# Attention with a learned position bias, then expert routing: set-up tables by single logarithms, loads of the second sequence spread out, the last result in halves

## The chip, the core and the metric

The kernel runs on one core of a Trainium2 chip. The metric is device time in microseconds (us) of one execution. The engines are TensorE (PE, with its weight loads as PEld), VectorE (DVE), ScalarE (ACT), GpSimd (POOL) and SyncE (SP). POOL and SP also issue transfers (DMAs), each into a queue of its own.

## What is computed

Eight sequences of 576 tokens with 8 heads of 64 go through attention. A small network of 32 hidden units makes a position bias for each pair (i, j), and the 4608 resulting rows of 512 go to one of 8 experts each:

```python
psi_rel = np.log1p(np.abs(pos[:, None] - pos[None, :]))
psi_i = np.log1p(np.maximum(pos[:, None], 1.0))
x = (psi_rel / psi_i)[..., None]
h = np.maximum(x @ w1 + b1, 0.0)
bias = h @ w2                                   # one bias per head
scores = q @ k.T / sqrt(64) + bias
x = softmax(scores) @ v                         # rows of 8 heads x 64
for e in range(8):                              # each row belongs to one expert
    out[mask_e] = np.maximum(x[mask_e] @ w1[e], 0.0) @ w2[e]
```

## The kernel before

The work has three stages. PE, DVE and ACT run in the order in which the code is written (a manual schedule); the order on POOL and SP is set by the scheduler from the order of the code and from dependences.

**Set-up and bias.** `_setup_constants` (L127 to L197) makes a table L4 of log(1+|distance|), 1075 columns for the first eight row groups and 636 columns (tile li1, `last_table`) for the ninth. POOL writes whole numbers by iota, ACT takes Abs (L168, L191) and then Ln (L174, L192). For each query row `slope` holds w1/log(1+i): DVE makes the whole numbers (L169, L171), ACT takes Ln (L173), and `slopes(a, b)` takes the reciprocal and multiplies by w1 (L177, L178): 16 columns ahead of the first row, the other 128 in the midst of the first group, after its eighth row. `nb1` (L183) is the negated b1. `G.zero` is a tile of zeros that DVE fills (L162); SP writes it over the whole scratch tensor fire_x (9252 KB, L277) after the second group. `_phase_bias` then runs nine groups (ib) of 16 rows. A hidden row `hr` (128 x 576) is one instruction, on DVE as multiply and maximum (L218) or on ACT as Relu (L215: five rows of sixteen in the first two groups, then three). PE multiplies the rows by W2BIG (L238, L243), and ACT takes exp of the sums into the bias tables (biasM, L256; biasR, L251; the ninth group L264).

**Attention.** A unit is a block of scores: PE makes the scores into one of two PSUM buffers (L564, L570), ACT takes exp (L593), DVE multiplies by the bias table (L604), PE multiplies by v (vext for the first 512 keys, L629; vrag for the last 64, L627). PLAN, a table in the code, sets which unit's products follow which scores. Loads go out on POOL's queue in the order of the code (`G.issue`): `load_qk` (qn, kn; 512 KB each), `load_v` (vst), `load_last` (the last 64 rows of q and k, four small transfers) and `load_vrag` (two small ones). `start()` loads sequences 0 and 1 whole. qn, kn and vst take slots of a pool of six (`G.n4`); a slot comes free when its tile has been read for the last time (for vst that is `make_vext`, the copy L502). POOL also loads expert weights (w, L752) and scatters finished rows into fire_x (L671).

**Experts.** For each expert PE makes the hidden layer (L841) and the output (L813, eight matmuls of 512 columns for 128 rows, into the PSUM tile ops), DVE copies ops to res (L820), and POOL scatters res to the output (L821). The very last block of 128 rows is copied as two parts, one by DVE (L817) and one by ACT (L818).

Of the kernel before, what the change touches and what calls it, by code (L numbers as in the profile page):

```python
# [128 lines left out]
def _setup_constants(tc, G, w1, b1, w2):  # L129

    nc = tc.nc
    cst = G.cst
    w1col = cst.tile([P, 1], F32, tag="w1col", name="w1col")
    nc.sync.dma_start(out=w1col, in_=bass.AP(tensor=w1.tensor, offset=0, ap=[[0, 4], [1, 32], [1, 1]]))  # L140
    G.pb1 = cst.tile([P, 1], F32, tag="pb1", name="pb1")
    nc.sync.dma_start(out=G.pb1, in_=bass.AP(tensor=b1.tensor, offset=0, ap=[[0, 4], [1, 32], [1, 1]]))
    nc.scalar.preload_act_table_set("natural_log_exp_and_others")
    w2f = cst.tile([P, 32], F32, tag="w2f", name="w2f")
    nc.vector.memset(w2f, 0.0)
    for g in range(4):
        nc.sync.dma_start(out=w2f[32 * g: 32 * g + 32, 8 * g: 8 * g + 8], in_=w2[:, :])
    li = G.tmp.tile([P, W4], I32, tag="li", name="li")
    nc.gpsimd.iota(li, base=-C4, channel_multiplier=0, pattern=[[1, W4]])
    si = G.tmp.tile([P, NGR], I32, tag="si", name="si")  # L150

    nc.gpsimd.iota(si[:, 0:128], base=0, channel_multiplier=0, pattern=[[1, 4], [16, 32]])
# [27 lines left out]
    G.slopes = slopes  # L180
# [7 lines left out]
    G.second_layer = second_layer  # L188

    def last_table():  # L190
        nc.scalar.activation(out=lf1, in_=li1, func=AF.Abs, bias=gs[:, 3:4], scale=1.0)  # L191
        nc.scalar.activation(out=G.L4[:, W4:], in_=lf1, func=AF.Ln, bias=1.0, scale=1.0)  # L192
    G.last_table = last_table
    G.idn = cst.tile([P, P], F16, tag="idn", name="idn")
    make_identity(nc, G.idn)


def _phase_bias(tc, G, route, at, x_dram):
# [3 lines left out]
    with tc.tile_pool(name="fsb", bufs=1, side="right") as fsb, \  # L202
         tc.tile_pool(name="fps", bufs=1, space=bass.MemoryType.PSUM) as fps:

        def hidden(ib):
            hrl = []
            for k16 in range(16):
                if ib < 8:
                    r, a = ib // 2, 16 * (ib % 2) + k16
                    m, c0 = 32 * r + a, C4 - (16 * a + r)  # L210
                else:
                    m, c0 = 128 + k16, W4 + C1 - 4 * k16
                hr = fsb.tile([P, S], F16, tag="hr", name="hr", bufs=34)
# [216 lines left out]
class _Attention:  # L430
# [47 lines left out]
    def load_last(self, b, xs="qk"):  # L478
        nc = self.nc
        for nm in xs:  # L480
            x, src = "qk".index(nm), self.q if nm == "q" else self.k
            for h2 in range(2):
                self.G.issue(nc.gpsimd.dma_start(
                    out=self.last[b % 2][64 * h2: 64 * h2 + 64, :, x, 64 * h2: 64 * h2 + 64],
                    in_=src[b, h2::2, 512:576, :].rearrange("h p d -> p h d")))

    def load_v(self, b):
        nc = self.nc
# [49 lines left out]
    def scores(self, b, u, sc=None):  # L538
# [54 lines left out]
        nc.scalar.activation(out=ef[:, 0:n], in_=sf[:, 0:n], func=AF.Exp, bias=0.0, scale=0.125)  # L593
        if bias is None or j == 0:
            return None
        if j == 1:
# [95 lines left out]
    def run(self, route, late):  # L692
# [25 lines left out]
        for n in range((B + 1) * NU):  # L718
# [86 lines left out]
def _phase_moe(tc, G, moe_w1, moe_w2, x_dram, out):  # L805
# [4 lines left out]
    def second(hT, t0, e, idx):  # L810
        ops_ = mps.tile([P, DM], F32, tag="ops", name="ops", bufs=2)
        for fc in range(8):
            nc.tensor.matmul(out=ops_, lhsT=hT[:, fc, t0: t0 + 128], rhs=G.w.w2(e, fc),  # L813
                             start=(fc == 0), stop=(fc == 7))
        res = msb.tile([P, DM], F32, tag="res", name="res", bufs=RES)
        if (e, t0) == (E - 1, CAP - 128):
            nc.vector.tensor_copy(out=res[:, 0:256], in_=ops_[:, 0:256])  # L817
            nc.scalar.copy(out=res[:, 256:], in_=ops_[:, 256:])  # L818
        else:
            nc.vector.tensor_copy(out=res, in_=ops_)  # L820
        inst = nc.gpsimd.indirect_dma_start(  # L821
            out=out[:], out_offset=bass.IndirectOffsetOnAxis(ap=idx.bitcast(I32), axis=0),
            in_=res[:], in_offset=None, bounds_check=NTOK - 1, oob_is_err=False)
# [42 lines left out]
    for e in range(E):  # L866
# [67 lines left out]
def kernel(  # L934
# [25 lines left out]
    with tc.manual_schedule(engines={ET.PE, ET.DVE, ET.Activation}):  # L960
        with ExitStack() as att:
# [69 lines left out]
```

## Time and profile before

| | us |
|---|---|
| median of 3 runs | 356.21 (355.79 to 356.76) |
| profiled execution, its own time | 355.02 |
| its span, first to last instruction | 353.5 |
| PE busy | 324.5 (92%) |
| DVE busy | 247.3 (70%) |
| ACT busy | 246.3 (70%) |
| POOL busy | 167.7 (47%) |
| mean granted TensorE clock | 0.972 |

The profile is of one execution. The table gives shares of the whole span; the stages differ, so that each has to be read from its own stretch: from the start to about 50 us the bias tables are made, from there to about 205 us attention runs, and after that the experts.

### The profile page before, as it was taken

The page shows a single profiled execution, that of the slowest core. Times are in us where ns is not written, and L with a number is a line of the kernel's source. Part 1 is how long each engine was busy: PE and PEld are TensorE (multiplying, and loading weights), DVE is VectorE, ACT ScalarE, POOL GpSimd, SP SyncE. Part 2 cuts the span into 40 slices and gives each one's busy share as a digit, 9 for nine tenths or more (in the row PEclk, how much of TensorE's full clock was granted, in tenths as well). Part 3 has the DMA queues.
Part 4 walks back from the last instruction along what each step waited for, and adds up shares of the span by engine and source line. Part 5 has one row for each costly group of instructions (what it writes and reads, how often), then busy time and mean ns, then how long its engine had stood idle before and what let it go on. Part 6 is the DMA issues. An engine that isn't in the chain of part 4 may idle for free. (4 is left out here: it accounts for less than half of the span.)

```text
span 353.5 us, 9881 instructions
## 1 busy us (share of the span) xinstructions
PE 324.5 (92%) x4218; PEld 213.4 (60%) x4218; DVE 247.3 (70%) x436; ACT 246.3 (70%) x299; POOL 167.7 (47%) x211
## 2 busy tenths in 40 slices
PE   0489888999999999999999899999999999999993
PEld 0478855766666676666675564565655555565651
DVE  7999998999999999999999861206163616161211
ACT  7999989999999999999999953241424232323330
POOL 8370004727687676958483622506051515151323
PEclk9999757999999999999999999999999999999998
DMA  3999999999999899999999543999999999980202
GB/s 43 195 158 345 352 341 213 192 194 163 167 128 192 115 190 111 200 101 200 149 202 220 129 71 93 283 323 230 322 206 325 248 289 264 271 322 32 114 32 107
DMA packets 89349, 69.20 MB, mean 196 GB/s; under 512 B 43605, under 2 KB 77653, under 8 KB 89304
## 3 DMA queue, kind: packets, MB, share of 16 engines
q0 software_dynamic: 51984, 37.26, 65.0%
q1 hardware_dynamic: 37320, 31.30, 32.7%
q8 instruction: 33, 0.54, 0.6%
q14 instruction: 12, 0.10, 0.1%
HBM read 61.93 MB, written 24.70 MB: 245 GB/s over the span
## 5 line engine op out<-in xcount | busy, mean ns | idle before, releaser
L593 ACT ACTIVATE e<-sc 128x1024 f16<-128x1024 f32 x157 | 148.2, 1059 | 1.7
L874 ACT ACTIVATE hT<-hps 128x640 f16<-128x640 f32 x56 | 39.4, 704 | 78.1 <-PE hps L841 77.8
L820 DVE COPY res<-ops 128x512 f32<-128x512 f32 x39 | 27.0, 692 | 91.1 <-PE ops L813 90.1
L821 POOL DMA_INDIRECT out_dram<-res,ids x40 | 44.9, 1123 | 89.8 <-DVE res L820 73.3
L604 DVE TENSOR_TENSOR e<-e,biasM 128x2048 f16<-128x2048 f16 x64 | 72.9, 1149 | 1.6 <-ACT e L593 1.5
L813 PE MATMUL ops<-w,hT 128*128 128x512 f16 x320 | 70.5, 379 | 0.0
L629 PE MATMUL pu<-vext,e 128*128 128x65 f16 (+1 forms) x1280 | 64.8, 194 | 0.0
L841 PE MATMUL hps<-xT,w 128*128 128x320 f16 x448 | 62.0, 299 | 0.0
L629 PEld LDWEIGHTS <-e 128*128 128x128 f16 (+1 forms) x1280 | 56.1, 101 | 8.8 <-issue 6.8
L841 PEld LDWEIGHTS <-w 128*128 128x128 f16 x448 | 43.8, 98 | 18.1
L813 PEld LDWEIGHTS <-hT 128*128 128x128 f16 x320 | 31.2, 98 | 36.5 <-ACT hT L853 0.3
L564 PE MATMUL sc<-qkT 64*128 64x512 f16 x252 | 49.7, 391 | 3.8 <-ACT e L593 3.6
L671 POOL DMA_INDIRECT fire_x<-xt,posi x32 | 40.1, 1253 | 15.3 <-issue 7.6
L218 DVE TENSOR_SCALAR hr<-L,slope,nb 128x576 f16<-128x576 f16 x113 | 41.4, 433 | 0.1
L238 PE MATMUL eb<-W2BIG,hr 128*128 128x32 f16 x576 | 24.0, 192 | 14.6 <-DVE W2BIG L187 10.1
L627 PE MATMUL pu<-vrag,e 128*128 128x130 f16 (+1 forms) x160 | 35.7, 223 | 0.2 <-ACT e L593 0.2
L238 PEld LDWEIGHTS <-hr 128*128 128x128 f16 x576 | 21.5, 115 | 17.8 <-POOL vrag L450 6.7
L215 ACT ACTIVATE hr<-L,pb,slope 128x576 f16<-128x576 f16 x31 | 24.6, 873 | 1.4 <-DVE nb L183 1.2
L671 POOL DMA_INDIRECT fire_x<-xl,posi x8 | 9.1, 1133 | 30.8 <-issue 13.8
L564 PEld LDWEIGHTS <-qkT 64*128 64x128 f16 x256 | 13.5, 93 | 16.3 <-issue 8.3
L643 DVE TENSOR_TENSOR xt<-pu,rz 128x512 f16<-128x512 f32 (+1 forms) x33 | 22.3, 675 | 1.5
L627 PEld LDWEIGHTS <-e 128*128 128x128 f16 (+1 forms) x160 | 16.0, 100 | 11.2 <-issue 6.6
(124 smaller groups left out, 352.5 us busy)
## 6 DMA issues: line engine op xcount, KB each, us to landing
st<-in_moe_w_dram SPq DMA_DIRECT2D x15, 1024.0 KB
fire_x<-zero SPq DMA_DIRECT2D x1, 9252.0 KB
w<-in_moe_w_dram POOLq DMA_DIRECT2D x17, 512.0 KB
qn<-in_q_dram POOLq DMA_DIRECT2D x8, 512.0 KB
kn<-in_k_dram POOLq DMA_DIRECT2D x8, 512.0 KB
vst<-in_v_dram POOLq DMA_DIRECT2D x8, 512.0 KB
out_dram<-res,ids POOLq DMA_INDIRECT x40
last<-zero SPq DMA_DIRECT2D x2, 256.0 KB
```

Source lines behind the costliest of these rows:

```text
L218: nc.vector.tensor_scalar(out=hr, in0=G.L4[:, c0: c0 + S], scalar1=G.slope[:, m: m + 1], scalar2=G.nb1[:], op0=AO.mult, op1=AO.max)
L238: nc.tensor.matmul(out=eb[:, lj, 32 * k16: 32 * k16 + 32], lhsT=rap(hr, jc, [[4, 128]]), rhs=G.W2BIG[:, 0:32], start=True, stop=True)
L564: mm(out=sc[:, h2, :], lhsT=self.qkT[b, p][hs[h2], 1, 128 * c: 128 * c + 128], rhs=self.qkT[b, p][hs[h2], 0, :], start=not raw, stop=True)
L593: nc.scalar.activation(out=ef[:, 0:n], in_=sf[:, 0:n], func=AF.Exp, bias=0.0, scale=0.125)
L604: self.nc.vector.tensor_tensor(out=job[0], in0=job[0], in1=job[1], op=AO.mult)
L627: mm(out=out, lhsT=last, rhs=vr[:, pair, :], start=True, stop=False, skip_group_check=True)
L629: mm(out=out[:, 65 * h2: 65 * h2 + 65], lhsT=keys[j], rhs=vx[:, 2 * pair + h2, j, :], start=False, stop=(h2 == 1 and j == 3), skip_group_c ...
L671: inst = self.nc.gpsimd.indirect_dma_start(out=self.x_dram[:, :], out_offset=bass.IndirectOffsetOnAxis(ap=self.G.posi[0:n, c:c + 1], axis= ...
L813: nc.tensor.matmul(out=ops_, lhsT=hT[:, fc, t0: t0 + 128], rhs=G.w.w2(e, fc), start=(fc == 0), stop=(fc == 7))
L821: inst = nc.gpsimd.indirect_dma_start(out=out[:], out_offset=bass.IndirectOffsetOnAxis(ap=idx.bitcast(I32), axis=0), in_=res[:], in_offset ...
L841: nc.tensor.matmul(out=hps[:, i, 0:HC], lhsT=G.w.w1(e, dc, fc), rhs=xT[:, dc, HC * hf: HC * hf + HC], start=(dc == 0), stop=(dc == 3))
L874: nc.scalar.activation(out=hT[:, fc, :].rearrange("p (a b) -> p a b", a=2), in_=first(e, xT, ((fc, 0), (fc, 1))), func=AF.Relu, bias=0.0, ...
```

## The change

1. Set-up. The tables come from Ln alone. The first is made in three pieces by ACT: the columns right of the diagonal with scale 1, the columns left of it with scale -1, and 12 columns at the diagonal from `md`, a tile of 15 columns whose absolute value DVE takes. The ninth group's table is made likewise (572, 3 and 61 columns). `slopes` is gone: all 144 slopes are inverted in one instruction and multiplied by w1 in another (now with two tensors as operands) ahead of the first row. `nb1` is made by multiplying two tensors. POOL instead of DVE writes the zeros of `G.zero`, and the iota of li1 is issued after the attention's tiles are made and ahead of the first load.
2. Loads. `start()` loads sequence 0 and q and k of sequence 1. The last rows of q and k of sequence 1 are loaded after unit (0, 0), with a wait for that unit's exp; v of sequence 1 goes out at unit (0, 6), its vrag at unit (0, 13).
3. The last block of 128 rows is made by 16 matmuls of 256 columns into the two halves of one PSUM tile (a buffer of hps). ACT copies the first half, DVE and ACT a quarter each of the rest, into one tile, and one scatter follows.

```diff
@@ set-up
-    nc.gpsimd.iota(li, base=-C4, channel_multiplier=0, pattern=[[1, W4]])
-    nc.gpsimd.iota(li1, base=-(C1 + 512), channel_multiplier=0, pattern=[[1, W1]])
+    nc.gpsimd.iota(mi, base=0, channel_multiplier=0, pattern=[[1, 12]])
+    up = C4 + 12
+    nc.gpsimd.iota(li[:, up:], base=up - C4, channel_multiplier=0, pattern=[[1, W4 - up]])
+    nc.gpsimd.iota(li[:, 0:C4], base=-C4, channel_multiplier=0, pattern=[[1, C4]])
...
-    nc.vector.memset(G.zero, 0.0)
-    nc.scalar.activation(out=lf, in_=li, func=AF.Abs, bias=gs[:, 2:3], scale=1.0)
...
-    nc.scalar.activation(out=G.L4[:, 0:W4], in_=lf, func=AF.Ln, bias=1.0, scale=1.0)
-    def slopes(a, b):
-        nc.vector.reciprocal(out=G.slope[:, a:b], in_=G.slope[:, a:b])
-        nc.vector.tensor_scalar(out=G.slope[:, a:b], in0=G.slope[:, a:b], scalar1=w1col[:], scalar2=None,
-                                op0=AO.mult)
-    slopes(0, 16)
+    nc.vector.tensor_scalar(out=md[:, 0:12], in0=mi, scalar1=gs[:, 1:2], scalar2=None, op0=AO.subtract)
+    nc.vector.tensor_scalar(out=md[:, 12:], in0=mi[:, 0:3], scalar1=gs[:, 0:1], scalar2=None, op0=AO.subtract)
+    nc.vector.scalar_tensor_tensor(out=md, in0=md, scalar=-1.0, in1=md, op0=AO.mult, op1=AO.max)
+    def ln(c0, c1, src, **kw):
+        nc.scalar.activation(out=G.L4[:, c0:c1], in_=src, func=AF.Ln, **kw)
+    ln(up, W4, li[:, up:], bias=gs[:, 2:3], scale=1.0)
+    ln(C4, up, md[:, 0:12], bias=1.0, scale=1.0)
+    ln(0, C4, li[:, 0:C4], bias=gs[:, 3:4], scale=-1.0)
+    nc.vector.reciprocal(out=G.slope, in_=G.slope)
+    nc.vector.tensor_tensor(out=G.slope, in0=G.slope, in1=w1col.to_broadcast([P, NGR]), op=AO.mult)
-    nc.vector.tensor_scalar(out=G.nb1, in0=G.pb1, scalar1=-1.0, scalar2=None, op0=AO.mult)
+    nc.vector.tensor_tensor(out=G.nb1, in0=G.pb1, in1=neg, op=AO.mult)
...
+    nc.gpsimd.memset(G.zero, 0.0)
@@ hidden(ib)
                 if (ib, k16) == (0, 7):
-                    G.slopes(16, NGR)
                     G.second_layer()
@@ loads
     def start(self):
-        for b in range(2):
-            self.load_qk(b)
-            self.load_v(b)
-            self.load_last(b)
-            self.load_vrag(b)
+        self.load_qk(0)
+        self.load_v(0)
+        self.load_last(0)
+        self.load_vrag(0)
+        self.load_qk(1)
...
+            if (b, ui) == (0, 0):
+                self.load_last(1, hold=self.exp)
             if b == 0 and ui in (3, 5):
                 self.load_qk(2, "q" if ui == 3 else "k")
+            if (b, ui) == (0, 6):
+                self.load_v(1)
+            if (b, ui) == (0, 13):
+                self.load_vrag(1)
@@ last block
-        if (e, t0) == (E - 1, CAP - 128):
-            nc.vector.tensor_copy(out=res[:, 0:256], in_=ops_[:, 0:256])
-            nc.scalar.copy(out=res[:, 256:], in_=ops_[:, 256:])
+    def second_last(hT, t0, e, idx):
+        ps = mps.tile([P, 2, 512], F32, tag="hps", name="hps", bufs=2)
+        res = G.n4("resl").bitcast(F32)[:, 0:DM]
+        for half in range(2):
+            for fc in range(8):
+                nc.tensor.matmul(out=ps[:, half, 0:256], lhsT=hT[:, fc, t0: t0 + 128],
+                                 rhs=G.w.w2(e, fc)[:, 256 * half: 256 * half + 256],
+                                 start=(fc == 0), stop=(fc == 7))
+        nc.scalar.copy(out=res[:, 0:256], in_=ps[:, 0, 0:256])
+        nc.vector.tensor_copy(out=res[:, 256:384], in_=ps[:, 1, 0:128])
+        nc.scalar.copy(out=res[:, 384:], in_=ps[:, 1, 128:256])
+        store(res, idx)
@@ main
+            G.last_columns()            # the iota of li1
             at.start()
```

The order on POOL at the start of the program, between its first iota and its first load. Before, from the last memsets of the set-up on (keep, less, ut belong to the routing, vrag and vext to the attention):

```order
L331 MEMSET keep 128x320
L335 MEMSET less_147 128x16
L336 MEMSET less_147 128x16
L448 MEMSET vrag_150 128x520
L332 MEMSET keep 128x8
L333 MEMSET keep 128x8
L467 MEMSET vext_162 128x32
L467 MEMSET vext_163 128x32
L474 DMA qn<-in_q_dram 128x8x256
L450 MEMSET vrag_150 64x4 x2
L474 DMA kn<-in_k_dram 128x8x256
L490 DMA vst<-in_v_dram 128x8x256
```

With the change, the iotas of the set-up with the memset of the zeros,

```order
L158 IOTA mi 128x12
L162 IOTA li 128x564
L163 IOTA li 128x499
masks.py:197 MEMSET idn 128x128
L216 MEMSET zero 128x2056
```

and, eleven short instructions later, the last ones ahead of the loads:

```order
L468 MEMSET vrag_160 128x520
L487 MEMSET vext_172 128x32
L487 MEMSET vext_173 128x32
L206 IOTA li_134 128x636
L470 MEMSET vrag_160 64x4 x2
L494 DMA qn<-in_q_dram 128x8x256
L494 DMA kn<-in_k_dram 128x8x256
L514 DMA vst<-in_v_dram 128x8x256
```

The memset of the zeros is new on this engine, the 636 columns of li1 have moved from the third place to just ahead of the loads, and the two small memsets of vrag now stand ahead of the load of qn instead of behind it.

The order of POOL's transfers behind those of sequence 0, with the change (a digit at a tile's name is its buffer, 169 and 161 those of sequence 1):

```order
L494 DMA qn<-in_q_dram 128x8x256 [waits DMASW1_49]
L494 DMA kn<-in_k_dram 128x8x256 [waits DMASW2_49]
L503 DMA last_169<-in_q_dram 64x4x64 [waits DMAHW1_49,DMASW3_49,Activation_49]
L503 DMA last_169<-in_q_dram 64x4x64 [waits DMASW4_49]
L503 DMA last_169<-in_k_dram 64x4x64 [waits DMASW5_49]
L503 DMA last_169<-in_k_dram 64x4x64 [waits DMASW6_49]
L494 DMA qn<-in_q_dram 128x8x256 [waits DMASW7_49]
L494 DMA kn<-in_k_dram 128x8x256 [waits DMASW0_49,DVE_49]
L514 DMA vst<-in_v_dram 128x8x256 [waits DMASW1_49,PE_49]
```

Before, qn and kn of sequence 1 were followed at once by vst, last and vrag of sequence 1, and only qn and kn of sequence 2 waited for DVE (the copy of vst) and for PE (the last transposes of qn). Now qn of sequence 2 finds a free slot, kn waits for DVE and vst of sequence 1 for PE; the five weight loads and then vrag of sequence 1 (two transfers) follow.

The copies at the very end, with the change, on ACT and then on DVE:

```order
L917 ACTIVATE hT<-hps 128x640 [waits PE_49,Activation_49]
L917 ACTIVATE hT<-hps 128x640 [waits PE_49] x7
L858 COPY resl<-hps 128x256 [waits DMAHW5_49,DMASW2_49,PE_49]
L860 COPY resl<-hps 128x128 [waits DVE_49]
```

```order
L846 COPY res<-ops 128x512 [waits DMASW1_49,DVE_49,PE_49]
L846 COPY res<-ops 128x512 [waits DMASW2_49,DVE_49,PE_49]
L859 COPY resl<-hps 128x128 [waits Activation_49]
```

Before, DVE copied its part once PE was done, and ACT waited for DVE. Now ACT begins, DVE waits for ACT, and ACT waits for DVE.

## Rows read from the trace of the kernel before

**Rows 1.** Busy time of each engine in three stretches (PE, PEld, DVE, ACT, POOL; clock):
```profile
40.00:50.00 10.00, 9.07 (x202) 7.24 (x201) 10.00 (x29) 8.49 (x14) 0.00 (x0) 0.51 1.11 338
...
120.00:205.00 85.00, 81.87 (x1363) 55.83 (x1361) 81.56 (x118) 84.32 (x95) 57.36 (x69) 1.00 1.07 166
205.00:349.00 144.00, 142.49 (x908) 82.71 (x908) 50.39 (x70) 46.89 (x64) 48.74 (x44) 1.00 0.82 214
```

**Rows 2.** Timeline, end of the bias stage (start, us, engine, line, idle before):
```profile
46.95 2.04 ACT L256 ACTIVATE biasM<-eb 128x1024 f16<-128x1024 f32 x2 [1.05 <-PE eb L238]
...
49.89 2.86 ACT L593 ACTIVATE e<-eb 128x1024 f16<-128x1024 f32 x3 [0.46 <-PE eb L570]
```

**Rows 3.** Timeline of DVE from 4 to 10 us:
```profile
4.09 1.57 DVE L178 TENSOR_SCALAR slope<-slope,w1col 128x16 f32<-128x16 f32 x1
...
5.24 0.42 DVE L183 TENSOR_SCALAR nb<-pb 128x1 f32<-128x1 f32 x1
...
5.79 2.96 DVE L218 TENSOR_SCALAR hr<-L,slope,nb 128x576 f16<-128x576 f16 x6
...
8.68 0.93 DVE L177 RECIPROCAL slope<-slope 128x128 f32<-128x128 f32 x1
...
9.85 0.18 DVE L187 TENSOR_SCALAR W2BIG<-w2f 128x32 f16<-128x32 f32 x1
```

**Rows 4.** Timeline of POOL from 2 to 7 us:
```profile
2.38 0.65 POOL L155 IOTA li<- 128x636 int32 x1
...
2.98 0.28 POOL masks.py:197 MEMSET idn<- 128x128 f16 x1
...
4.71 0.52 POOL L448 MEMSET vrag<- 128x520 f16 x1
...
5.26 0.37 POOL L467 MEMSET vext<- 128x32 f16 x2
5.38 1.09 POOL L474 DMA_DIRECT2D qn<-in_q_dram  x1
...
6.46 0.50 POOL L450 MEMSET vrag<- 64x4 f16 x2
```

**Rows 5.** Timeline of DVE, thirteen hidden rows in two groups:
```profile
21.97 4.93 DVE L218 TENSOR_SCALAR hr<-L,slope,nb 128x576 f16<-128x576 f16 x13
...
27.02 4.52 DVE L218 TENSOR_SCALAR hr<-L,slope,nb 128x576 f16<-128x576 f16 x13
```

**Rows 6.** Timeline of POOL, the load of v of sequence 1:
```profile
22.46 0.93 POOL L490 DMA_DIRECT2D vst<-in_v_dram  x1
```

**Rows 7.** Timeline of POOL, transfers issued in the first sequence, and a wait for one:
```profile
57.86 0.88 POOL L474 DMA_DIRECT2D kn<-in_k_dram  x1 [3.63 <-PE pt L505]
...
66.45 1.63 POOL L752 DMA_DIRECT2D w<-in_moe_w_dram  x2 [1.97 <-DMA kn<-in_k_dram]
...
80.72 1.03 POOL L671 DMA_INDIRECT fire_x<-xt,posi  x1 [1.07 <-DMA w<-in_moe_w_dram]
```

**Rows 8.** Timeline, first uses of the last rows, of v and of vrag of sequence 1:
```profile
61.04 0.38 PE L505 MATMUL ptl<-idn,last 128*128 128x128 f16 x4 [0.37 <-DMA last<-in_k_dram]
...
74.45 0.69 DVE L502 COPY vext<-vst 128x2048 f16<-128x2048 f16 x1
...
80.69 0.23 PE L627 MATMUL pu<-vrag,e 128*128 128x130 f16 x1
```

**Rows 9.** DMA queues from 34 to 44 us (packets, MB, share of 16 engines):
```profile
q1 hardware_dynamic: 755, 3.10, 81.9%
q0 software_dynamic: 754, 0.39, 27.8%
```

**Rows 10.** Timeline of the end of the program:
```profile
347.98 0.43 DVE L817 COPY res<-ops 128x256 f32<-128x256 f32 x1 [1.04 <-PE ops L813]
348.44 0.37 ACT L818 COPY res<-ops 128x256 f32<-128x256 f32 x1 [8.39 <-DMA out_dram<-res,ids]
349.09 0.98 POOL L821 DMA_INDIRECT out_dram<-res,ids  x1 [0.88 <-POOLq L901]
```

More of the change, by code (lines that the diff above doesn't have):

```diff
@@ L100, in _ins, with _behind @@
     return inst.ins if hasattr(inst, "ins") else inst
+def _behind(tc, inst, before):
+    tc.add_manual_dep(_ins(inst), before.name, mybir.DependencyInfo(
+        mybir.DependencyClass.Sync, mybir.DependencyReason.DATA), reason="paced")
 class _Issue:
@@ L147, in _setup_constants @@
         nc.sync.dma_start(out=w2f[32 * g: 32 * g + 32, 8 * g: 8 * g + 8], in_=w2[:, :])
-    li = G.tmp.tile([P, W4], I32, tag="li", name="li")
-    nc.gpsimd.iota(li, base=-C4, channel_multiplier=0, pattern=[[1, W4]])
     si = G.tmp.tile([P, NGR], I32, tag="si", name="si")
@@ L153, in _setup_constants @@
     nc.gpsimd.iota(si[:, 128:144], base=512, channel_multiplier=0, pattern=[[4, 16]])
-    li1 = G.bsb.tile([P, W1], I32, tag="li1", name="li1")
-    nc.gpsimd.iota(li1, base=-(C1 + 512), channel_multiplier=0, pattern=[[1, W1]])
-    gs = cst.tile([P, 4], F32, tag="gs", name="gs")
+    mi = cst.tile([P, 12], I32, tag="mi", name="mi")
+    nc.gpsimd.iota(mi, base=0, channel_multiplier=0, pattern=[[1, 12]])
+    li = G.tmp.tile([P, W4], I32, tag="li", name="li")
+    up = C4 + 12
+    nc.gpsimd.iota(li[:, up:], base=up - C4, channel_multiplier=0, pattern=[[1, W4 - up]])
+    nc.gpsimd.iota(li[:, 0:C4], base=-C4, channel_multiplier=0, pattern=[[1, C4]])
+    gs = cst.tile([P, 6], F32, tag="gs", name="gs")
     for g in range(4):
         nc.vector.memset(gs[32 * g: 32 * g + 32, 0:1], float(g))
-    for i, f in ((2, -4.0), (1, 4.0), (3, -1.0)):
-        nc.vector.tensor_scalar(out=gs[:, i: i + 1], in0=gs[:, 0:1], scalar1=f, scalar2=None, op0=AO.mult)
-    nc.vector.memset(G.zero, 0.0)
-    lf = G.tmp.tile([P, W4], F32, tag="lf", name="lf")
-    lf1 = li1.bitcast(F32)
+    for i, f, o in ((1, 4.0, 0.0), (2, -4.0, 1.0), (3, 4.0, 1.0), (4, -1.0, 1.0), (5, 1.0, 1.0)):
+        nc.vector.tensor_scalar(out=gs[:, i: i + 1], in0=gs[:, 0:1], scalar1=f, scalar2=o,
+                                op0=AO.mult, op1=AO.add)
+    neg = cst.tile([P, 1], F32, tag="neg", name="neg")
+    nc.vector.memset(neg, -1.0)
     G.L4 = G.bsb.tile([P, W4 + W1], F16, tag="L4", name="L4")
     G.slope = G.bsb.tile([P, NGR], F32, tag="slope", name="slope")
-    nc.scalar.activation(out=lf, in_=li, func=AF.Abs, bias=gs[:, 2:3], scale=1.0)
     nc.vector.tensor_scalar(out=G.slope[:, 0:128], in0=si[:, 0:128], scalar1=gs[:, 1:2], scalar2=1.0,
@@ L173, in _setup_constants @@
     nc.scalar.activation(out=G.slope, in_=G.slope, func=AF.Ln, bias=1.0, scale=1.0)
-    nc.scalar.activation(out=G.L4[:, 0:W4], in_=lf, func=AF.Ln, bias=1.0, scale=1.0)
-    def slopes(a, b):
-        nc.vector.reciprocal(out=G.slope[:, a:b], in_=G.slope[:, a:b])
-        nc.vector.tensor_scalar(out=G.slope[:, a:b], in0=G.slope[:, a:b], scalar1=w1col[:], scalar2=None,
-                                op0=AO.mult)
-    G.slopes = slopes
-    slopes(0, 16)
+    md = cst.tile([P, 15], F32, tag="md", name="md")
+    nc.vector.tensor_scalar(out=md[:, 0:12], in0=mi, scalar1=gs[:, 1:2], scalar2=None, op0=AO.subtract)
[8 more added lines that the diff above has]
+    nc.vector.tensor_tensor(out=G.slope, in0=G.slope, in1=w1col.to_broadcast([P, NGR]), op=AO.mult)
     G.nb1 = cst.tile([P, 1], F32, tag="nb1", name="nb1")
-    nc.vector.tensor_scalar(out=G.nb1, in0=G.pb1, scalar1=-1.0, scalar2=None, op0=AO.mult)
+    nc.vector.tensor_tensor(out=G.nb1, in0=G.pb1, in1=neg, op=AO.mult)
     G.W2BIG = G.bsb.tile([P, 32], F16, tag="W2BIG", name="W2BIG")
@@ L188, in _setup_constants, with last_columns @@
     G.second_layer = second_layer
+    li1 = G.bsb.tile([P, W1], I32, tag="li1", name="li1")
+    mid = C1 + 512
+    def last_columns():
+        nc.gpsimd.iota(li1, base=-(C1 + 512), channel_multiplier=0, pattern=[[1, W1]])
+    G.last_columns = last_columns
     def last_table():
-        nc.scalar.activation(out=lf1, in_=li1, func=AF.Abs, bias=gs[:, 3:4], scale=1.0)
-        nc.scalar.activation(out=G.L4[:, W4:], in_=lf1, func=AF.Ln, bias=1.0, scale=1.0)
+        ln(W4, W4 + mid, li1[:, 0:mid], bias=gs[:, 5:6], scale=-1.0)
+        ln(W4 + mid, W4 + mid + 3, md[:, 12:], bias=1.0, scale=1.0)
+        ln(W4 + mid + 3, W4 + W1, li1[:, mid + 3:], bias=gs[:, 4:5], scale=1.0)
     G.last_table = last_table
@@ L476, in load_qk, with load_last @@
             self.nat[b, nm] = t
-    def load_last(self, b, xs="qk"):
+    def load_last(self, b, xs="qk", hold=None):
         nc = self.nc
@@ L482, in load_last @@
             for h2 in range(2):
-                self.G.issue(nc.gpsimd.dma_start(
+                inst = nc.gpsimd.dma_start(
                     out=self.last[b % 2][64 * h2: 64 * h2 + 64, :, x, 64 * h2: 64 * h2 + 64],
-                    in_=src[b, h2::2, 512:576, :].rearrange("h p d -> p h d")))
+                    in_=src[b, h2::2, 512:576, :].rearrange("h p d -> p h d"))
+                if hold is not None:
+                    _behind(self.tc, inst, _ins(hold))
+                    hold = None
+                self.G.issue(inst)
     def load_v(self, b):
@@ L592, in scores @@
         ef, sf = e.rearrange("p a i -> p (a i)"), sc.rearrange("p a i -> p (a i)")
-        nc.scalar.activation(out=ef[:, 0:n], in_=sf[:, 0:n], func=AF.Exp, bias=0.0, scale=0.125)
+        self.exp = nc.scalar.activation(out=ef[:, 0:n], in_=sf[:, 0:n], func=AF.Exp, bias=0.0, scale=0.125)
         if bias is None or j == 0:
@@ L815, in second, with store @@
         res = msb.tile([P, DM], F32, tag="res", name="res", bufs=RES)
-        if (e, t0) == (E - 1, CAP - 128):
-            nc.vector.tensor_copy(out=res[:, 0:256], in_=ops_[:, 0:256])
-            nc.scalar.copy(out=res[:, 256:], in_=ops_[:, 256:])
-        else:
-            nc.vector.tensor_copy(out=res, in_=ops_)
+        nc.vector.tensor_copy(out=res, in_=ops_)
+        store(res, idx)
[10 more added lines that the diff above has]
+        nc.scalar.copy(out=res[:, 384:], in_=ps[:, 1, 128:256])
+        store(res, idx)
+    def store(res, idx):
         inst = nc.gpsimd.indirect_dma_start(
             out=out[:], out_offset=bass.IndirectOffsetOnAxis(ap=idx.bitcast(I32), axis=0),
-            in_=res[:], in_offset=None, bounds_check=NTOK - 1, oob_is_err=False)
+            in_=res, in_offset=None, bounds_check=NTOK - 1, oob_is_err=False)
         G.issue.scatter(inst)
@@ L887, in _phase_moe @@
                 first_rest(hT, xT)
-            second(hT, 128 * kk, e, ids[:, kk, :])
+            (second_last if (e, kk) == (E - 1, NCH - 1) else second)(hT, 128 * kk, e, ids[:, kk, :])
         if 0 < e < E - 1:
```

## The prediction

> **What bounds the kernel now.** I read the stages first, then in each stage the wait that ends last. From 120 to 205 us ACT is busy 84.32 of 85 us, and in the expert stage PE is busy 142.49 of 144 [rows 1]. Nothing in the change takes work off ACT in the one or off PE in the other, except in the very last block. So both stages keep their length, and what counts is when attention starts, and the tail. The bias stage ahead of attention is paced by DVE: from 40 to 50 us DVE is busy all 10.00 us while ACT has 8.49 [rows 1], and ACT waits 1.05 us for a sum of PE before its exp at 46.95 and 0.46 us before the first exp of attention [rows 2]. Whatever DVE gains or loses before 46 us, ACT passes on; ACT could follow a gain of about 1.05 us by its own slack, and more since its Abs passes go.
>
> A measurement of this kernel can tell a change of about 0.3%, here 1.07 us, from none.
>
> **The change part by part.**
>
> *Slopes ahead of the first row.* The reciprocal of 128 slopes and its product stand today between two hidden rows, from 8.68 us to the W2BIG product at 9.85 [rows 3]: 1.17 us that leaves DVE's busy stretch. Their successors, 144 columns in one reciprocal (0.93 us for 128 columns [rows 3], so some 1.05) and one product, run ahead of the first row, where DVE today waits anyhow: nb starts only at 5.24, when its vector has landed [rows 3]. That part costs nothing and gives **-1.17**.
>
> *When the first row starts.* This is the term that decides. Today the product of only 16 columns takes 1.57 us, from 4.09 to 5.66, and nb behind it also ends at 5.66 [rows 3]; the 32 columns of W2BIG, the same kind of instruction, take 0.18 [rows 3]. POOL meanwhile runs instruction after instruction without a gap, and its last memset (vext) ends at 5.63 [rows 4]. So I read: such a DVE instruction waits as long as POOL's instructions follow one another, through some ten of them, and gets in when the streak ends. The two products themselves are tensor-by-tensor in the change and I take them as free of this; the hidden row (L218) is of the kind that waited. The change makes POOL's streak longer. It adds the memset of 2056 columns of zeros: 0.28 us for 128 columns and 0.52 for 520 [rows 4] give 0.61 ns a column and 1.46 us; in proportion to the 520 columns it would be 2.06; I take 1.7, between them. Two more small instructions (the 12-column iota, the table's iota in two) at 0.06 each, half of the 0.12 from vext's start to the load's [rows 4], add 0.12. The iota of 636 columns (0.65) only moves inside the streak. The streak then ends at 5.38 + 0.12 + 1.7 = 7.2 us, and the first row gets in there instead of at 5.79: **+1.4**. With 1.46 or 2.06 it is +1.15 or +1.75. If an iota does not hold DVE up (no row here shows one alone doing so), the row gets in 0.65 earlier, +0.75. A gain, if nothing holds it, is the first rival below.
>
> *Loads beside the rows.* Six rows take 2.89 us, from 5.79 to 8.68 [rows 3], against 4.52 for thirteen in an undisturbed group [rows 5], or 0.35 each: 0.8 us goes to the loads of qn, kn and vst that POOL issues just then. They come as close behind the first row as today, so this stays. The load of v of sequence 1 [rows 6] leaves the bias stage; the group around it took 4.93 instead of 4.52 [rows 5], with kn's end and vst in it. Vst's part is between 0 and 0.41; I take 0.25, over half: **-0.25**.
>
> DVE's sum is -1.17 + 1.4 - 0.25 = -0.02: what the slopes give, POOL's longer streak takes back.
>
> *ACT's set-up.* Without Abs the tables are made in less time, ahead of 5.5 us; DVE's rows and not ACT's decide, so 0.
>
> *The loads that move.* POOL's queue now stands at the last rows of sequence 1 until the first exp, about 50.9 (a third of the 2.86 us behind 49.89 [rows 2]). What is behind it, qn and kn of sequence 2, is not read before the second sequence; today kn goes out only at 57.86 [rows 7]. Last then needs four issues; today it is used at 61.04, where PE waited 0.37 us for it [rows 8] without ACT noticing. Now it starts with the fill of the scratch tensor nearly done: today the fill (q1) has 81.9% of the transfer engines and the loads of sequence 1 (q0) 27.8% beside it [rows 9]; without them the fill ends several us earlier. V takes the place of kn at 57.86, since both wait for a slot that PE frees. Today kn lands at 66.45, 8.6 us after its issue [rows 7], so v lands by 66.4 against a use at 74.45 [rows 8]: 0. The weights behind it land by 80.72 today [rows 7], 14.3 us after kn; with v landing at 63 to 66.4, the last of them lands at 77.3 to 80.7, and vrag 0.5 to 1 us later, 78 to 81.7. Its first use is at 80.69 [rows 8], and ACT has up to two blocks of scores in hand, about 0.95 each by rows 2. I take 0; the second rival is the case in which this is late.
>
> *The tail.* Today DVE's copy starts at 347.98 and ACT's ends at 348.81 [rows 10]: 0.43, 0.03, 0.37. In the change the three copies wait for one another and the first for all sixteen matmuls, since only the last of these signals: 0.37, and twice a handover of 0.03 with a copy of 128 columns, which I put at 0.28 (between half of 0.37 and all of it). That is 0.99 for 0.83, **+0.16**; -0.04 to +0.34 by these bounds. The sixteen matmuls of 256 columns have the columns of eight of 512, and weight loads, 82.71 us beside 142.49 [rows 1], have room: 0.
>
> **Sum:** -1.17 + 1.4 - 0.25 + 0.16 = +0.14 us. The profiled execution took 355.02 us, so 355.16 on its own scale; it stands 1.19 under the median of the runs. On the median's scale 356.21 + 0.14, or **356.4 us**. The case's own range: down to 355.1 (short memset, iota not holding, the most from vst), up to 357.3 (long memset, nothing from vst, the dearest tail).
>
> **Rivals.**
>
> *A, the row does not wait for the streak.* The first row waits for one POOL instruction at most and then the rows follow each other on DVE while POOL's memsets take their turn. For it: two memsets of vrag fall at 6.46 into the rows [rows 4], and the six rows need no more than the loads explain. Against it: the 1.57 us of L178 across some ten POOL instructions. The first row would start at about 5.5 (nb's vector lands at 5.24, then nb and a short hold), 0.25 earlier than today: -1.17 - 0.25 - 0.25 + 0.16 = -1.5, or **354.7 us**, faster.
>
> The Trainium skill, "SBUF — State Buffer", section "Who interferes with whom", says that of such a VectorE instruction and a GpSimd instruction whoever issues first holds a shared port pair for that whole instruction and the other is blocked until it ends; by its letter the wait is one instruction long, which is this rival. The trace agrees on the blocking, and its 1.57 us speaks for a longer one.
>
> *B, vrag of sequence 1 lands late.* Place: the product at 80.69 [rows 8]. PE works in order, so scores behind it stop, and ACT runs dry after its two blocks. It decides from a landing at about 82.6 on; each us behind that costs one. For it: the upper end of the estimate is 81.7, and last, vrag and weights share one queue. Against it: the fill ends early. At 84.6, about 3 us beyond that upper end, it costs 2 us and the time is **358.4 us**, slower.
>
> *C, the halves overlap.* If ACT copied the first half while PE makes the second, only the last two copies would stand behind PE, and not even both in a row if ACT and DVE work side by side: about 0.3 to 0.6 instead of 0.83, and **355.8 us**, which can't be told from no change. Against it: the waits, by which the first copy follows the last matmul.
>
> **Chances.** Forecast 0.58, A 0.28, B 0.09, C 0.05. Faster by over 0.3% is A and a sliver of the forecast's low end, 0.30; slower is B and a sliver of its high end, 0.11; within 0.3% is the rest, 0.59. The range runs from 354.4 (A with a somewhat larger gain) to 357.4 (the forecast's high end), and leaves out B and little else.
>
> **What would show it.** In the profile after: POOL's memset of the zeros at 1.5 to 2.1 us and its load of qn at 7 to 7.7; DVE's first hidden row ending at about 7.5 (right) or at 6 (rival A); no reciprocal after it; W2BIG at 10 or so; ACT's first exp of attention at 49.9 as today, or over 1 us earlier if A holds; no wait of ACT near 81 us; three copies one after the other at the end. The forecast is wrong if attention starts more than 1 us off today's place, or if ACT shows waits between 60 and 205 us.

## The result: slower by 0.7%, from one small load

| | before | after |
|---|---|---|
| median of 11 runs, us | 355.66 (354.03 to 356.76) | 357.82 (356.35 to 358.66) |
| ratio to before | | 1.0072 (1.0052 to 1.0092) |
| profiled execution, us | 355.02 | 358.49 |
| its span, us | 353.5 | 356.9 |

In brackets stand the lowest and the highest run, and for the ratio its 95% interval. The profiled execution of the changed kernel lies at the upper end of its runs: its span shows 3.4 us where the medians differ by 2.2.

**The stage that lost.** Busy time by stretches, first of the kernel before, then two of the profile after (columns as in [rows 1]):

```profile
60.00:120.00 60.00, 58.60 (x979) 39.87 (x978) 57.88 (x85) 59.17 (x66) 39.26 (x50) 1.00 1.17 163
```

```profile
60.00:120.00 60.00, 56.97 (x924) 38.42 (x923) 54.33 (x79) 55.66 (x63) 36.65 (x50) 0.94 1.20 167
120.00:205.00 85.00, 82.13 (x1362) 55.77 (x1359) 81.97 (x118) 84.35 (x95) 59.80 (x71) 1.00 1.08 165
```

From 120 to 205 us ACT is as busy as in [rows 1]. Between 60 and 120 us it is idle for 4.3 us, before for 0.8. The timeline of PE and ACT near 80 us says why (start, us, engine, line, idle before):

```profile
79.73 0.39 PE L588 MATMUL sc<-qkT 64*128 64x512 f16 x2
82.61 0.27 PE L651 MATMUL pu<-vrag,e 128*128 128x130 f16 x1 [2.48 <-DMA vrag<-in_v_dram]
...
83.45 1.04 PE L594 MATMUL sc<-qkT,qkTl 128*128 128x512 f16 x2
```

```profile
75.69 5.61 ACT L617 ACTIVATE e<-sc 128x1024 f16<-128x1024 f32 x6
84.53 2.12 ACT L617 ACTIVATE e<-sc 128x1024 f16<-128x1024 f32 x2 [3.23 <-PE sc L594]
87.05 5.06 ACT L617 ACTIVATE e<-sc 128x1024 f16<-128x1024 f32 x5 [0.40 <-PE sc L588]
```

PE stands 2.48 us at the first product with vrag of sequence 1, the use of [rows 8]. The next scores are behind it in PE's order, and ACT runs dry at 81.30 for 3.23 us, then for 0.40. This is the second rival. Its tracks on POOL:

```profile
52.86 1.25 POOL L503 DMA_DIRECT2D last<-in_q_dram  x2 [30.33 <-ACT e L617]
...
55.30 0.93 POOL L494 DMA_DIRECT2D qn<-in_q_dram  x1
...
56.19 0.92 POOL L494 DMA_DIRECT2D kn<-in_k_dram  x1
...
57.64 0.88 POOL L514 DMA_DIRECT2D vst<-in_v_dram  x1 [0.53 <-PE pt L529]
...
58.51 1.26 POOL L503 DMA_DIRECT2D last<-in_q_dram  x2
...
59.73 1.26 POOL L503 DMA_DIRECT2D last<-in_k_dram  x2
...
60.94 1.86 POOL L782 DMA_DIRECT2D w<-in_moe_w_dram  x2
64.70 0.75 POOL L782 DMA_DIRECT2D w<-in_moe_w_dram  x1 [1.91 <-DMA kn<-in_k_dram]
68.09 1.63 POOL L782 DMA_DIRECT2D w<-in_moe_w_dram  x2 [2.64 <-DMA vst<-in_v_dram]
...
69.94 1.25 POOL L521 DMA_DIRECT2D vrag<-in_v_dram  x2
```

POOL waits at the last rows of sequence 1 until 52.86. Only then q and k of sequence 2 go out. V behind them lands at about 68: the weight load that waits for it starts at 68.09. Behind v come the last rows of sequence 2, four small transfers that the account of the change passes over, and five weights of 512 KB. Vrag, issued at 69.94, is there 12.7 us later.

**The stage that was forecast to decide.** The start, on DVE and POOL:

```profile
2.73 1.81 POOL L216 MEMSET zero<- 128x2056 f16 x1
...
5.51 3.16 DVE L239 TENSOR_SCALAR hr<-L,slope,nb 128x576 f16<-128x576 f16 x6
...
6.20 0.62 POOL L468 MEMSET vrag<- 128x520 f16 x1
6.76 0.54 POOL L487 MEMSET vext<- 128x32 f16 x2
6.89 0.94 POOL L206 IOTA li<- 128x636 int32 x1
...
8.13 1.10 POOL L494 DMA_DIRECT2D qn<-in_q_dram  x1
...
8.59 0.62 DVE L199 TENSOR_SCALAR W2BIG<-w2f 128x32 f16<-128x32 f32 x1
```

The first row did not wait for POOL's streak: it starts at 5.51 while POOL still has eleven instructions to run ahead of its first load. DVE and POOL then slow each other. Six rows take 3.16 us, though a load falls only on the last of them, where an undisturbed six take 2.1 by [rows 5]; the same memset of vrag takes 0.62 instead of 0.52 and the iota 0.94 instead of 0.65 [rows 4]. The two products that are now tensor by tensor were not held up, as assumed: 0.31 us for the slopes at 4.10 and 0.16 for nb at 5.24, beside the same streak. At W2BIG DVE is 1.26 us ahead of [rows 3]; then the loads of q, k and v, which came beside the first six rows before, come beside later ones. What is left at the end:

```profile
46.76 2.05 ACT L276 ACTIVATE biasM<-eb 128x1024 f16<-128x1024 f32 x2 [1.05 <-PE eb L258]
...
49.72 2.85 ACT L617 ACTIVATE e<-eb 128x1024 f16<-128x1024 f32 x3 [0.46 <-PE eb L594]
```

Attention starts 0.17 us earlier than in [rows 2]. The tail, to be read against [rows 10]:

```profile
351.30 0.37 ACT L858 COPY resl<-hps 128x256 f32<-128x256 f32 x1 [7.95 <-PE hps L855]
351.70 0.29 DVE L859 COPY resl<-hps 128x128 f32<-128x128 f32 x1 [1.46 <-ACT resl L858]
352.03 0.27 ACT L860 COPY resl<-hps 128x128 f32<-128x128 f32 x1 [0.36 <-DVE resl L859]
352.57 0.98 POOL L864 DMA_INDIRECT out_dram<-resl,ids  x1 [1.06 <-POOLq L944]
```

From the first copy to the scatter 1.27 us, before 1.11: +0.16. In sum, -0.17 + 3.23 + 0.40 + 0.16 = 3.6 us, against 3.4 in the spans.

### The profile page after: what moved, and what is told of

Read it like the earlier page. It is cut to its first block, busy times and chain, and to the rows that moved or that the text cites. A ratio compares the mean times of both kernels' runs of the same rounds, so it can differ in the third digit from the quotient of the medians.

```text
span 356.9 us, 9900 instructions
## 1 busy us (share of the span) xinstructions
PE 327.4 (92%) x4226; PEld 215.5 (60%) x4226; DVE 246.7 (69%) x439; ACT 246.1 (69%) x302; POOL 168.8 (47%) x214
## 5 line engine op out<-in xcount | busy, mean ns | idle before, releaser
L864 POOL DMA_INDIRECT out_dram<-res,ids x39 | 44.0, 1128 | 88.8 <-DVE res L846 72.7
L843 PE MATMUL ops<-w,hT 128*128 128x512 f16 x312 | 68.8, 379 | 0.0
L653 PE MATMUL pu<-vext,e 128*128 128x65 f16 (+1 forms) x1280 | 65.8, 196 | 0.0
L653 PEld LDWEIGHTS <-e 128*128 128x128 f16 (+1 forms) x1280 | 57.0, 101 | 9.3 <-issue 7.5
L843 PEld LDWEIGHTS <-hT 128*128 128x128 f16 x312 | 30.4, 98 | 35.5 <-ACT hT L896 0.3
L695 POOL DMA_INDIRECT fire_x<-xt,posi x32 | 38.8, 1214 | 14.5 <-issue 7.6
L239 DVE TENSOR_SCALAR hr<-L,slope,nb 128x576 f16<-128x576 f16 x113 | 42.7, 446 | 0.1
L258 PE MATMUL eb<-W2BIG,hr 128*128 128x32 f16 x576 | 24.9, 192 | 13.2 <-DVE W2BIG L199 9.3
L503 POOL DMA_DIRECT2D last<-in_q_dram x16 | 10.5, 693 | 30.3 <-ACT e L617 30.3
L651 PEld LDWEIGHTS <-e 128*128 128x128 f16 (+1 forms) x160 | 16.1, 101 | 13.7 <-issue 6.6
```

The costliest lines, as they stand in the source:

```text
L239: nc.vector.tensor_scalar(out=hr, in0=G.L4[:, c0: c0 + S], scalar1=G.slope[:, m: m + 1], scalar2=G.nb1[:], op0=AO.mult, op1=AO.max)
L258: nc.tensor.matmul(out=eb[:, lj, 32 * k16: 32 * k16 + 32], lhsT=rap(hr, jc, [[4, 128]]), rhs=G.W2BIG[:, 0:32], start=True, stop=True)
L651: mm(out=out, lhsT=last, rhs=vr[:, pair, :], start=True, stop=False, skip_group_check=True)
L653: mm(out=out[:, 65 * h2: 65 * h2 + 65], lhsT=keys[j], rhs=vx[:, 2 * pair + h2, j, :], start=False, stop=(h2 == 1 and j == 3), skip_group_c ...
L695: inst = self.nc.gpsimd.indirect_dma_start(out=self.x_dram[:, :], out_offset=bass.IndirectOffsetOnAxis(ap=self.G.posi[0:n, c:c + 1], axis= ...
L864: inst = nc.gpsimd.indirect_dma_start(out=out[:], out_offset=bass.IndirectOffsetOnAxis(ap=idx.bitcast(I32), axis=0), in_=res, in_offset=No ...
```

## The experiments

The theory: vrag of sequence 1, behind five weights in POOL's queue, costs all of the loss; set-up and tail are worth nearly nothing. Rivals: the moved loads as a whole fill the queue, so that some load is late whichever comes last; PE's lower clock costs it; the set-up or the tail does. For the bias stage a mark is used below: the start of DVE's copy of biasW (L260 before, L280 after) behind the 100th hidden row.

### The change taken apart

*a_vrag_early*, the change with vrag ahead of the weights:

```diff
             if (b, ui) == (0, 6):
                 self.load_v(1)
+                self.load_vrag(1)
-            if (b, ui) == (0, 13):
-                self.load_vrag(1)
```

> The changed kernel with the vrag of sequence 1 issued right behind its v, ahead of the weights (unit (0, 6) instead of (0, 13)). Theory (late vrag): the wait of PE for vrag (2.48 us at 82.61 in the trace after) and that of ACT behind it (3.23 and 0.40) are gone; attention ends 3.4 to 3.6 us earlier than with the change and the time is 0.1 to 0.4 us under the kernel before (ratio 0.999 to 1.0). Rival (the loads that moved fill the queue, whichever comes last): v and vrag now push the weights and the last rows of sequence 2 back, another load is late, and the ratio stays at 1.005 to 1.01. Rival (clock): the half clock of PE from 81.5 to 88.4 us is there all the same and costs about 1 us, ratio 1.002 to 1.004.

*b_loads_only*, the kernel before with part 2 of the change alone:

> The kernel before with the loads of the change alone. Theory (late vrag): the same wait of PE near 80 us, about 2.3 us, ACT idle some 3.2 us; +3.0 to +3.6 us in the profile, ratio 1.008 to 1.010. Rival (set-up or tail cost it): no more than 1 us slower, ratio under 1.003.

*c_setup_only*, with part 1 alone:

> The kernel before with the set-up of the change alone. Theory: attention's first exp 0.1 to 0.3 us earlier than before, nothing else, ratio 0.999 to 1.0: the 1.17 us of slopes and the 0.28 us of the earlier first row are taken back by POOL's streak and by transfer issues between the rows. Rival (the set-up's gain was lost to the moved loads): first exp 0.8 us earlier or more, ratio 0.997 to 0.998. Rival (the set-up costs): ratio over 1.002.

*d_tail_only*, with part 3 alone:

> The kernel before with the last block in halves alone. Theory: three copies in a row, last scatter 0.1 to 0.3 us later against PE's end, ratio 1.0 to 1.001. Rival (halves overlap): 0.2 to 0.4 us earlier, ratio 0.999.

| | median, us | ratio to before (before here 354.68) |
|---|---|---|
| a_vrag_early | 354.98 | 1.0004 (0.9989 to 1.0019) |
| b_loads_only | 357.61 | 1.0082 (1.0057 to 1.0107) |
| c_setup_only | 355.38 | 1.0006 (0.9989 to 1.0023) |
| d_tail_only | 355.07 | 1.0002 (0.9988 to 1.0016) |

The loads alone make the loss, and moving two small transfers takes it away. The product with vrag in a_vrag_early, without a wait, and in b_loads_only:

```profile
79.88 0.23 PE L651 MATMUL pu<-vrag,e 128*128 128x130 f16 x1
```

```profile
82.29 0.22 PE L636 MATMUL pu<-vrag,e 128*128 128x130 f16 x1 [2.14 <-DMA vrag<-in_v_dram]
```

In a_vrag_early ACT waits nowhere between 58 and 205 us, so no other load takes the place of vrag. In b_loads_only ACT waits 2.76 and 0.17.

The lower clock comes with the wait. Stretches of the profile after, then of a_vrag_early (the clock is the third number from the end):

```profile
76.00:80.00 4.00, 4.00 (x64) 2.56 (x62) 3.94 (x7) 4.00 (x5) 0.82 (x2) 1.00 1.26 207
80.00:84.00 4.00, 1.52 (x18) 1.15 (x17) 2.80 (x3) 1.31 (x2) 2.56 (x3) 0.69 1.02 77
84.00:88.00 4.00, 4.00 (x38) 2.11 (x36) 1.46 (x3) 3.00 (x3) 3.39 (x5) 0.50 1.25 169
```

```profile
84.00:88.00 4.00, 3.94 (x73) 3.01 (x72) 3.97 (x7) 4.00 (x6) 3.61 (x3) 1.00 1.30 195
```

While PE stands for vrag its clock falls: the granted clock is 1.00 from 80 to 81 us, 0.77 from 81 to 82, and 0.50, the 1.2 GHz level, from 82 to 88. From 84 to 88 us it does 38 matmuls where it does 73 without the wait. The products and scores behind vrag ran at that clock, and ACT started again only 1.92 us after vrag was there (82.61 to 84.53). With the wait gone the low clock is gone too. So the clock is no cause by itself, but it adds to the price; how much, *i_no_hold* shows below.

The set-up alone moves the mark from 46.53 to 46.57, the loads alone to 46.23, the whole change to 46.33. Attention starts at 49.94 with the set-up alone, 0.05 us later than before, where 0.1 to 0.3 earlier was expected. The tail alone takes 1.26 us from the first copy to the scatter, against 1.11 before; in the times that can't be told from nothing.

d_tail_only's profile showed that the kernel before has a late load of its own. The last rows of sequence 1, for which PE waited 0.37 in [rows 8] without ACT noticing, came later in this execution, and ACT stood 0.96 and 0.77 us. The execution was the slowest of its 13 (356.99 us), so the lateness is not in all of them:

```profile
61.92 0.38 PE L505 MATMUL ptl<-idn,last 128*128 128x128 f16 x4 [1.14 <-DMA last<-in_k_dram]
```

### How late, and by what

*e_vrag_12*, the change with vrag one place earlier, ahead of the fifth weight:

```diff
-            if (b, ui) == (0, 13):
+            if (b, ui) == (0, 12):
                 self.load_vrag(1)
```

> The changed kernel with the vrag of sequence 1 issued one place earlier, ahead of the fifth weight load and behind four (unit (0, 12)). Theory (place in the queue: each weight of 512 KB in front costs its transfer, about 2.6 us by the landings of the five weights in the trace after): vrag lands near 79.8 instead of 82.4, PE waits 0 to 0.5 us for it and ACT no more than 0.5; ratio 1.000 to 1.002. Rival (vrag is late because POOL stands at the last rows of sequence 1 until 52.9 us, or because of its own many small packets): it lands less than 1 us earlier, PE still waits 1.5 us or more, ratio 1.004 or more.

*i_no_hold*, the change without the wait at the last rows:

```diff
-                self.load_last(1, hold=self.exp)
+                self.load_last(1)
```

> The changed kernel without the wait of the last rows of sequence 1 for an exp (their place in POOL's order stays, and vrag stays behind the five weights). Theory (the hold is what makes the queue late: POOL stands at it until 52.9 us, so q and k of sequence 2 go out at 55.3 and 56.2 and are still in the queue ahead of v when v is issued at 57.6): q of sequence 2 goes out before 30 us, k at about 53, v lands near 63 instead of 67.8, the five weights by 76 to 77, vrag at 77 to 78; no wait of PE for vrag, ratio 0.999 to 1.0015. Rival (the place behind five weights alone is enough to make it late): vrag lands at 81 or later, PE waits 1 us or more, ratio 1.003 or more. Against both: the fill of the scratch tensor ends some us later than with the hold, since last rows and q of sequence 2 share the transfer engines with it.

e_vrag_12: 355.12 us, ratio 0.9992 (0.9972 to 1.0012). The product comes without a wait, ACT waits 0.2. One weight less in front of vrag is enough, as the theory of the place in the queue had it:

```profile
79.86 0.23 PE L651 MATMUL pu<-vrag,e 128*128 128x130 f16 x1
```

i_no_hold: 355.73 us, ratio 1.0018 (0.9998 to 1.0038). Neither side was right:

```profile
25.02 1.02 POOL L494 DMA_DIRECT2D qn<-in_q_dram  x1
53.26 0.88 POOL L494 DMA_DIRECT2D kn<-in_k_dram  x1 [27.21 <-DVE used L389]
57.70 0.87 POOL L514 DMA_DIRECT2D vst<-in_v_dram  x1 [3.56 <-PE pt L529]
...
66.75 1.63 POOL L782 DMA_DIRECT2D w<-in_moe_w_dram  x2 [1.87 <-DMA vst<-in_v_dram]
```

```profile
81.00 0.22 PE L651 MATMUL pu<-vrag,e 128*128 128x130 f16 x1 [0.76 <-DMA vrag<-in_v_dram]
```

```profile
82.12 4.69 ACT L617 ACTIVATE e<-sc 128x1024 f16<-128x1024 f32 x5 [0.70 <-PE sc L594]
```

q of sequence 2 goes out at 25, k at 53.26, and still v lands only at 66.7 and not near 63. One explanation is that the loads share the transfer engines with the fill of the scratch tensor again, as in [rows 9]. The queues agree: from 52 to 56 us the fill has 86.5% of the engines and the loads 26.4% beside it, where in the profile after the fill has 34.3%. It was not tried by itself. PE waits 0.76 us instead of 2.48, ACT 0.70. So the hold costs about 1.7 us of PE's wait for vrag, and the place behind five weights the rest; taking away either the hold alone or the last weight leaves little.

The run also prices the clock. PE's clock stays at 1.00 here, and ACT starts again 1.12 us after vrag is there (81.00 to 82.12). The same products and scores took 1.92 us at the lower clock, so of ACT's 3.23 us about 0.8 is the clock's by estimate.

### The set-up and the tail, improved

*f_zero_dve*, a_vrag_early with the zeros written by DVE as before:

```diff
     nc.vector.memset(neg, -1.0)
+    nc.vector.memset(G.zero, 0.0)
...
-    nc.gpsimd.memset(G.zero, 0.0)
```

> The kernel of a_vrag_early with the zeros written by DVE again (ahead of the slopes). Theory (POOL's longer streak takes back what the slopes give: six rows took 3.16 us in the trace after where thirteen undisturbed ones take 4.52, so 1.1 us, and W2BIG 0.4): POOL's streak ends 1.7 us earlier, the first rows run with the loads' stalls alone, and the first exp of attention comes 0.5 to 0.9 us earlier than the 49.53 of a_vrag_early; ratio to before 0.997 to 0.9985. Rival (the transfer issues between the rows take it, with or without the streak): less than 0.2 us earlier, ratio 0.999 to 1.0005. Rival (DVE's own 0.9 us for the zeros delays the first row): attention no earlier or later.

*g_tail_split*, a_vrag_early with a PSUM tile for each half:

```diff
-        ps = mps.tile([P, 2, 512], F32, tag="hps", name="hps", bufs=2)
         for half in range(2):
+            ps = mps.tile([P, 2, 512], F32, tag="hps", name="hps", bufs=2)
...
+            (nc.vector.tensor_copy if half else nc.scalar.copy)(
+                out=res[:, 256 * half: 256 * half + 256], in_=ps[:, 0, 0:256])
```

> The kernel of a_vrag_early with the last block's halves in two PSUM tiles: ACT copies the first while PE makes the second, DVE copies the second whole. Theory (one PSUM tile made all three copies wait for the last matmul): the last scatter starts 0.5 to 0.6 us earlier against the end of PE than in a_vrag_early, and 0.35 to 0.45 us earlier than before; ratio 0.9985 to 0.9995. Rival (the copies wait for something else): as in a_vrag_early.

*h_all*, both, and *j_all_no_hold*, both and no hold:

> All three: vrag early, zeros on DVE, halves in two PSUM tiles. Theory: the gains of f_zero_dve and g_tail_split add, ACT follows within its 1.05 us of slack; 0.9 to 1.5 us faster than before, ratio 0.996 to 0.9975. Rival (ACT or another engine takes over as the bound of the bias stage): about 0.4 us, ratio 0.999.

> The kernel of h_all without that wait. Theory (in h_all no load is late any more, so an earlier queue is worth nothing): as h_all, ratio 0.993 to 0.996. Rival (the loads are still close to their uses and the earlier queue takes away what waits are left): below 0.993. Rival (the small transfers beside the rows of the bias stage slow DVE again): 0.997 or more.

The last two once more, side by side:

> The kernel of h_all once more, unchanged, since j_all_no_hold came out 0.4% slower than it in another set of runs. If the hold of the last rows is what made that difference, this one repeats 0.993 to 0.9955. If the difference was between sets of runs, it comes out between, 0.995 to 0.998. Either way it should be faster than the kernel before.

> The kernel of j_all_no_hold once more beside k_all_again on the same chip. If the hold matters, it is 0.3 to 0.4% slower than k_all_again; if not, the two agree within 0.2%.

| | median, us | before, us | ratio |
|---|---|---|---|
| f_zero_dve | 354.32 | 355.31 | 0.9969 (0.9954 to 0.9984) |
| g_tail_split | 354.81 | 355.31 | 0.9985 (0.9968 to 1.0002) |
| h_all | 353.57 | 355.31 | 0.9940 (0.9923 to 0.9957) |
| j_all_no_hold | 354.57 | 354.89 | 0.9982 (0.9966 to 0.9998) |
| k_all_again | 353.94 | 355.17 | 0.9965 (0.9948 to 0.9982) |
| l_j_again | 354.51 | 355.17 | 0.9978 (0.9960 to 0.9997) |

f_zero_dve gains, and DVE shows it: the mark comes 1.07 us earlier than in a_vrag_early (first row below f_zero_dve, second a_vrag_early):

```profile
45.09 0.27 DVE L280 CAST biasW<-eb 128x128 f16<-128x128 f32 x1
```

```profile
46.16 0.28 DVE L280 CAST biasW<-eb 128x128 f16<-128x128 f32 x1
```

So the memset on POOL took back what the slopes gave. The first row starts no earlier (5.52 us, after 5.51), though POOL is done and at its first load by 5.84 instead of 8.13; what is gained comes in the rows behind.

Attention follows only in part, and in f_zero_dve's profile by far less than the expected 0.5 us. Its first exp is at 49.45 there, 48.89 in h_all and 48.42 in k_all_again, with the same set-up and marks within 0.05 us, against 49.53 in a_vrag_early. ACT has hardly any slack left to follow DVE with: in k_all_again it runs from 5.33 to 44.55 us without a wait. In the other two it also waits for sums of PE on the way: 0.45 us before 36.42 in h_all, 0.32 before 33.60 and 0.47 before 36.72 in f_zero_dve. Why those sums come later in one execution than in another these runs do not show.

g_tail_split missed. The copies do overlap, but the scatter hardly comes earlier:

```profile
347.89 0.37 ACT L857 COPY resl<-hps 128x256 f32<-128x256 f32 x1 [7.08 <-PE hps L854]
...
348.76 0.42 DVE L857 COPY resl<-hps 128x256 f32<-128x256 f32 x1 [1.05 <-PE hps L854]
349.95 0.98 POOL L862 DMA_INDIRECT out_dram<-resl,ids  x1 [0.99 <-POOLq L942]
```

From DVE's copy, the first behind PE's end, to the scatter 1.19 us: 0.08 less than after, 0.08 more than in [rows 10]. The copy ends 0.77 us before the scatter starts, and 0.77 or 0.78 in the four other profiles with this tail; with one releaser, as in the tail after, it was 0.27. Here the scatter waits for both ACT and DVE, which may be the cause; it was not tried apart. A tail that gives back 0.08 us can't carry h_all's gain, so most of it must be the set-up's. Why h_all gained more than f_zero_dve in the same set of runs is not shown.

h_all and k_all_again are one kernel, 0.35% to 0.6% faster than before in two sets of runs: the version to keep. j_all_no_hold missed its 0.993 to 0.996. In its profile the mark is 0.56 us later than in h_all, as the rival with the small transfers beside the rows would have it, but in l_j_again only 0.10 later than in k_all_again. Side by side the time without the hold is 0.16% longer, with intervals that overlap. Both pairs point the same way, but a gain from the hold there is not shown.

## Why the prediction was wrong

- **Attention keeps its length: failed at one place.** The step was the paragraph on the loads that move, "78 to 81.7 ... I take 0". Vrag was there at 82.6, and the term put at 0 cost ACT 3.6 us. What was off lay all to the same side. POOL stood at the held load until 52.86 and not 50.9: three units are issued ahead of the loop, so the exp that it waits for is the third, not the first. So the queue was not empty when v went out at 57.64; q and k had been issued just before, and v landed 10.4 us later, not 8.6 at most. And the use came at 80.12 instead of 80.69, with 1.2 us in ACT's hands (81.30) instead of 1.9. The weights and vrag behind v took 14.5 us, close to the forecast's 14.8 to 15.3. That part was right.
- **Rival B was the right mechanism, with the wrong chance and threshold.** It was to decide from a landing at 82.6 on; at 82.6 it had already cost 3.6 us of ACT. The step that was missing is what comes after the landing: PE first does the products that it was stopped at and then the scores (1.12 us at the full clock, 1.92 at the lower one), so that ACT's idle time (3.23) is longer than PE's (2.48). A landing estimated one us after a use, at the upper end of a range, deserved far more than 0.09.
- **The first row: the wrong mechanism, and a sum that came out about right by luck.** The forecast had it wait until 7.2 (+1.4). It started at 5.51, as rival A had it. But rows and POOL's instructions then slowed each other, and the loads came beside later rows. The set-up alone moved the mark by +0.04 where -1.17 + 1.4 = +0.23 was forecast; so what the forecast booked on one wait of 1.4 was about 1.2 us in several places. f_zero_dve shows that 1.07 of it hangs on the memset, which ran 1.81 us against 1.7 assumed.
- **What DVE gains, ACT passes on:** not in every execution. Of the 1.07 us that DVE gained in f_zero_dve 0.08 reached the start of attention; with the same set-up it was 0.64 in h_all and 1.11 in k_all_again.
- **The load of v beside the rows:** -0.25 forecast, -0.30 by the mark in b_loads_only. Right in size, though there the last rows and vrag of sequence 1 leave the stage with v, and v's share was not tried by itself.
- **The tail:** +0.16 forecast and measured, by three copies in a row. Right, as was ruling out rival C.
- **The range:** its terms add up to a high end of 357.1, not 357.3. The kernel before came out at 355.66 in the eleven runs instead of 356.21, so the forecast of +0.14 stands against a measured +2.16.
- **The Trainium skill's rule** ("SBUF — State Buffer", "Who interferes with whom") is that, of a VectorE instruction in a mode that uses the ports shared with GpSimd and an instruction of GpSimd, whoever issues first has them for the whole instruction and the other is blocked until it ends. A wait of one instruction at most, as rival A had it, fits the start of the rows after (5.51, amid POOL's streak) better than the forecast did. The 1.57 us of [rows 3], which spoke against it, is not explained by it.

## What to carry to other kernels

When a load is moved later, list everything that its queue then has ahead of it, with the time at which the queue's engine is really free to issue, and hold the landing against the use; a margin under 2 us with a stage at 99% behind it is a risk to be priced, not a zero. A late input of an in-order engine can cost more than the wait that it shows, here 3.6 us of ACT for 2.48 of PE: the work behind it, and here the clock, add to it. Small loads with an early use go ahead of large ones with a late use.

## What was not expected of the hardware

- PE's clock fell from 1.00 to 0.50 during a stand of 2.48 us that began at 80.1 us, stayed there until 88 us, and was at 1.00 again from 89 us on; without the stand it remained at 1.00.
- DVE's rows and POOL's memsets and iotas slow each other while both run: six rows 3.16 instead of 2.1 us, the iota of 636 columns 0.94 instead of 0.65. In f_zero_dve, where most of POOL's work is done before the rows start, the memset of vrag is back at 0.52 and the iota at 0.77.
